# Retention and two feed-forward layers in one kernel: the opening's state summed in a PSUM bank, and its first sums of squares by products with ones

## Chip, cores and metric

The kernel runs on one core of one Trainium2 chip. The metric is the device time of one execution in microseconds; the time of a kernel is the median of three such runs. PE is TensorE, ACT ScalarE, DVE VectorE, POOL GpSimd, SP the queue that issues most DMAs.

## What is computed

Four batches of 576 positions and eight heads of 64 go through retention (attention without softmax, with a decay matrix). The result, 2304 tokens of 512 features, is normalised by its root mean square and goes through two feed-forward layers. All of it is float32.

```python
scores = scale * np.matmul(q, k.transpose(0, 1, 3, 2))
ret = scores * Dmat[None]                       # gamma ** (i - j), lower triangle
x = np.matmul(ret, v)                           # -> (2304, 512)
xn = x / np.sqrt(np.mean(x * x, -1, keepdims=True) + 1e-06) * rms_g
h = silu(xn @ w_gate) * (xn @ w_val) @ w_out    # 512 -> 1536 -> 512
g = h @ w_in                                    # 512 -> 2048
out = np.where(g >= 1, g, np.where(g <= -1, 0, (g + 1) ** 2 / 4)) @ moe2_w_out
```

## The kernel before

**Retention** works on chunks of 128 positions, five in a batch (the fifth has 64), 20 in all. `scores` (line 412) forms the scores of a chunk within itself: 16 products into two PSUM banks, which DVE multiplies with the decay into the tiles `ret` (in the opening every second chunk uses the tiles `t0`, `t1` instead), while POOL scales q and k into `qs` and `ks`. `values` (line 439) forms the chunk's output x in a bank: products of the running `state` with `qs` for c > 0 ("state products"), then of v with `ret` ("x products"), and in a second bank the products of `ks` with v ("new-state products"). For c = 0 ACT copies these into `state`; for c > 0 DVE adds them to it (line 469). ACT copies x into `xraw` and squares it into `sq`; POOL adds the squares of the four feature groups into `sums` (lines 483 and 484).

**The norm** of a token block (`rms_rstd`, line 500) multiplies `sums` with a matrix of ones on PE, so that every partition holds the sum, takes the reciprocal root on ACT (`y`), and refines it on DVE (`m`, `e`, then `y`, in the tile `o`). `norm` multiplies `xraw` by it, and `split_x` splits it into a high and a low float32r part in `xall` (ACT casts, DVE subtracts). Products of the layers are made of three float32r products of such parts (`three`, line 536). The first layer has five token blocks of 12 steps (`step_a`, line 580): two groups of 12 products into the `fr` banks, the gate on ACT and DVE, and 12 products of the step before into the four `acc` banks. The layers' weights arrive as 64-bit words and are converted once (`convert`, line 275: ACT, a shift on DVE, a merge on DVE), written back to DRAM, and split into `wt`.

**The opening** (lines 778 to 793) runs `scores` of chunks 0 to 7 and `values` of chunks 0 to 6, one behind; after `values` of chunk 3, when block 0 (512 tokens) is complete, it puts `rms_rstd`, `norm` and `split_x` of block 0. It takes its banks from a list of three pairs, `at0`/`at1`, `acc0`/`acc1`, `acc2`/`acc3`. The weights of steps 0 and 1 are converted in the opening too. From step 0 on, `att_step` puts the other chunks between the groups of `step_a`, with the banks `at0` and `at1`.

**The order of the work** on each engine is set before the kernel runs: `Plan` takes every operation with its operands, gives it an estimated cost and a due time, and lists them (`issue`, line 139); PE prefers the order of the program, the others the earliest due time. A changed operation can therefore move others on every engine. Each engine then works its list strictly in that order, waiting for semaphores. As all operations are issued by one line, the profile names line 135 throughout; tiles tell them apart.

Of the kernel before, what the change touches and what calls it, by code (L numbers as in the profile page):

```python
# [10 lines left out]
F32 = mybir.dt.float32  # L11
# [9 lines left out]
P = 128  # L21
KD = DM // P
# [3 lines left out]
CH = 128  # L26
# [185 lines left out]
def moe_chain_kernel(ctx: ExitStack, tc: tile.TileContext, att, tail, wa, wb, dmat, gq, gk, out):  # L212
    nc = Plan(tc.nc)
# [12 lines left out]
    t_p = pool("t", 2)  # L226
    r_p = pool("r", 1)
    sum_p = pool("sum", 2)
    sq_p = pool("sq", 1)
    ps_p = pool("ps", 1, space=PSUM)  # L230
    fr_p = pool("fr", 2, space=PSUM)
    dram_p = pool("dram", 1, space=DRAM)
# [5 lines left out]
    ones = const.tile([P, P], F32, name="ones")  # L238
# [150 lines left out]
    def used(i):  # L389
        del att_t[i]  # L390
        while load_att():
            pass
# [43 lines left out]
            nc.vector.tensor_mul(out=ret[h][:n, :, :n], in0=ps[h][:n, :, :n], in1=d[:n, :, h, :n])  # L436
        used(2 * i)

    def values(tags):

        i = nvalued[0]
        nvalued[0] += 1
# [19 lines left out]
            )  # L462
        if c < NFULL:
            for u, h, r in heads:
                nc.tensor.matmul(new[r, u], lhsT=ks[:, 2 * u + h], rhs=v[:, 2 * u + h], start=True, stop=True)
            for h in range(2):
                r = slice(h * D, (h + 1) * D)
                if c:
                    nc.vector.tensor_add(out=state[r, :, r], in0=state[r, :, r], in1=new[r])
                else:  # L470
                    nc.scalar.copy(out=state[r, :, r], in_=new[r])
        g0 = b * S + c * CH
        for t, s0 in enumerate(STARTS):
            lo, hi = max(g0, s0), min(g0 + n, s0 + BLOCKS[t])
            if lo < hi:
                xs, ss = x_slice(t)
                m = hi - lo
                dst = slice(lo - s0, hi - s0)
                sq = sq_p.tile([P, NPAIR, CH], F32, tag="sq", name="sq")
                src = x[:, :, lo - g0:hi - g0]  # L480
                nc.scalar.copy(out=xs[:, :, dst], in_=src)
                nc.scalar.activation(out=sq[:, :, :m], in_=src, func=ACTF.Square)
                nc.gpsimd.tensor_add(out=sq[:, :2, :m], in0=sq[:, :2, :m], in1=sq[:, 2:, :m])
                nc.gpsimd.tensor_add(out=ss[:, dst], in0=sq[:, 0, :m], in1=sq[:, 1, :m])
        used(2 * i + 1)

    def att_step(goal, what):

# [11 lines left out]
    def rms_rstd(t, ps):  # L500

        T = BLOCKS[t]
        m, e, y = rms_tiles(T)
        nc.tensor.matmul(ps[:, :T], lhsT=ones, rhs=sums[t][:, :T], start=True, stop=True)
        nc.scalar.activation(out=y, in_=ps[:, :T], func=ACTF.Abs_reciprocal_sqrt, scale=1.0 / DM, bias=eps)
        nc.vector.tensor_scalar(out=m, in0=ps[:, :T], scalar1=1.0 / DM, scalar2=EPS, op0=ALU.mult, op1=ALU.add)
        nc.scalar.activation(out=e, in_=y, func=ACTF.Square)
        nc.vector.scalar_tensor_tensor(out=e, in0=e, scalar=-0.5, in1=m, op0=ALU.mult, op1=ALU.mult)
        nc.vector.scalar_tensor_tensor(out=y, in0=e, scalar=1.5, in1=y, op0=ALU.add, op1=ALU.mult)
        return y  # L510
# [56 lines left out]
    rms = {}  # L567
# [208 lines left out]
            nc.tensor.matmul(warm[:, :P], lhsT=ones, rhs=ones, start=True, stop=True)  # L776

    warm_up(WARM)
    tags = [("at0", "at1"), ("acc0", "acc1"), ("acc2", "acc3")] * ahead
    for i in range(ahead + 1):  # L780
        scores(tags.pop())
        if i:
            values(tags.pop())
        if nvalued[0] == first and not rms:
            rms["y"] = y = rms_rstd(0, fr_p.tile([P, 512], F32, tag="fr"))
            for k in range(KD):
                norm(0, k, k + 1, y)
                split_x(0, k, k + 1)
        if i in (1, first):
            weights_f32(0 if i == 1 else 1)  # L790
        if i == first - 1:
            weights_split(0, 0)
            weights_split(0, 1)
# [88 lines left out]
```

## Time and profile before

| | us |
|---|---|
| median of three runs (921.75 to 924.12) | 923.54 |
| the profiled execution, own time | 922.58 |
| its span, first to last instruction | 920.5 |
| PE busy | 905.2 (98%) |
| DVE busy | 575.6 (63%) |
| ACT busy | 478.4 (52%) |
| POOL busy | 70.7 (8%) |

The page gives busy times as shares of the whole span. POOL's 70.7 us all lie in the first 400 us. The granted clock of PE is 0.998 on average. The chain that ended last consists to 94% of PE.

### The profile page before, as it was taken

How to read it: one execution, taken by the hardware profiler on the slowest of the kernel's cores; microseconds unless marked ns; L12 is line 12 of the kernel's file. 1: busy time of each engine (PE TensorE's matmuls, PEld its weight loads, DVE VectorE, ACT ScalarE, POOL GpSimd, SP SyncE). 2: the span in 40 equal slices, each digit the busy share in tenths (PEclk: the TensorE clock that was granted, in tenths of full speed). 3: DMA queues.
4: the chain of work that ended last, by engine and by line, in shares of the span. 5: the costliest groups of instructions: out<-in, count | busy, mean ns of one | idle time of the engine just before them, and what ended most of it. 6: DMA issues, size and time to landing. Idle time of an engine off the chain costs nothing.

```text
span 920.5 us, 13316 instructions
## 1 busy us (share of the span) xinstructions
PE 905.2 (98%) x5098; PEld 798.2 (87%) x5098; DVE 575.6 (63%) x925; ACT 478.4 (52%) x852; POOL 70.7 (8%) x80
## 2 busy tenths in 40 slices
PE   7799999999999999999999999999999999999998
PEld 7578888888889999888899998989898998989896
DVE  3978988888888798854658545333744345434343
ACT  2447656555755655533555454545654455644443
POOL 4720100210013020100000000000000000000000
PEclk9999999999999999999999999999999999999999
DMA  9778887988859847653355387555765454756432
GB/s 362 234 265 294 293 307 255 395 301 300 313 185 396 330 141 259 257 196 104 103 178 177 104 307 264 205 172 189 268 232 194 171 193 167 266 166 213 159 137 69
DMA packets 51647, 209.94 MB, mean 228 GB/s; under 512 B 5632, under 2 KB 11392, under 8 KB 47488
## 3 DMA queue, kind: packets, MB, share of 16 engines
q1 hardware_dynamic: 45392, 199.51, 61.1%
q10 hardware_dynamic: 6192, 9.59, 2.8%
q8 instruction: 40, 0.66, 0.3%
q14 instruction: 23, 0.19, 0.1%
HBM read 167.14 MB, written 41.94 MB: 227 GB/s over the span
## 4 chain that ended last, share of the span: by engine, by line
PE 94%; DVE 3%; DMA 1%; ACT 1%; issue 1%; POOL 0%; ACTq 0%; DVEq 0%
PE fr L135 51%; PE acc L135 31%; PE at L135 12%; DMA att<-in_att_dram 1%; DVE xraw L135 1%; DVE xall L135 0%; DMA gk_sb<-in_gk_dram 0%; DVE w L135 0%; DVE t L135 0%; DVE wt L135 0%; DVE o L135 0%; DVE state L135 0%; ACT att L135 0%; ACT L135 0%; ACT sq L135 0%
## 5 line engine op out<-in xcount | busy, mean ns | idle before, releaser
L135 PE MATMUL fr<-xall,wt 128*128 128x384 f32 (+1 forms) x2424 | 512.5, 356 | 2.0 <-DVE xall L135 1.3
L135 PEld LDWEIGHTS fr<-xall,wt 128*128 128x128 f32 x2424 | 437.3, 188 | 51.9 <-DVE xall L135 2.4
L135 PE MATMUL acc<-h,wt 128*128 128x512 f32 (+1 forms) x708 | 159.4, 371 | 0.0
L135 PE MATMUL acc<-wprep,h 128*128 128x512 f32 x576 | 155.7, 394 | 0.5 <-ACT h L135 0.5
L135 PEld LDWEIGHTS acc<-h,wt 128*128 128x128 f32 x708 | 128.3, 188 | 18.3
L135 DVE TENSOR_TENSOR wt<-w,wt 128x1024 fp32r<-128x1024 f32 (+1 forms) x118 | 115.8, 993 | 25.6 <-ACT wt L135 25.1
L135 ACT CAST wt<-w 128x1024 fp32r<-128x1024 f32 (+1 forms) x118 | 96.9, 835 | 52.6 <-PE acc L135 29.6
L135 PEld LDWEIGHTS acc<-wprep,h 128*128 128x128 f32 x576 | 106.6, 188 | 15.8 <-ACT h L135 0.9
L135 DVE TENSOR_TENSOR t<-fr,t 128x512 f32<-128x512 f32 (+1 forms) x120 | 76.3, 636 | 55.7 <-PE fr L135 29.0
L135 ACT ACTIVATE att<-att 128x384 f32<-128x384 f32 x156 | 79.1, 523 | 30.8 <-DVE att L135 17.2
L135 ACT CAST h<-t 128x512 fp32r<-128x512 f32 (+1 forms) x60 | 34.6, 577 | 89.8 <-DVE t L135 89.7
L135 DVE TENSOR_TENSOR att<-fr,att 128x384 f32<-128x384 f32 x48 | 26.7, 555 | 71.0 <-ACT att L135 69.6
L135 PE MATMUL at<-wprep,h 128*128 128x512 f32 x288 | 70.3, 392 | 0.0
L135 DVE TENSOR_TENSOR h<-att,h 128x384 fp32r<-128x384 f32 x96 | 52.8, 554 | 23.5 <-ACT h L135 23.1
L135 PEld LDWEIGHTS at<-wprep,h 128*128 128x128 f32 x288 | 53.7, 188 | 10.4
L135 ACT COPY att<-fr 128x384 f32<-128x384 f32 x48 | 23.0, 479 | 75.8 <-PE fr L135 72.4
L135 ACT CAST h<-att 128x384 fp32r<-128x384 f32 x96 | 48.6, 511 | 21.3 <-DVE att L135 19.9
L135 ACT ACTIVATE t<-fr 128x512 f32<-128x512 f32 (+1 forms) x60 | 33.3, 554 | 49.5 <-PE fr L135 49.4
L135 DVE SCALAR_TENSOR_TENSOR att<-att,att 128x384 f32<-128x384 f32 x48 | 26.8, 558 | 40.9 <-ACT att L135 40.9
L135 DVE TENSOR_TENSOR h<-t,h 128x512 fp32r<-128x512 f32 (+1 forms) x60 | 38.1, 635 | 12.8 <-ACT h L135 12.6
L135 DVE SCALAR_TENSOR_TENSOR att<-att,fr 128x384 f32<-128x384 f32 x24 | 13.3, 553 | 35.8 <-ACT att L135 35.8
L135 DVE TENSOR_TENSOR xall<-xraw,xall 128x512 fp32r<-128x512 f32 (+2 forms) x32 | 26.0, 828 | 2.6 <-ACT xall L135 2.4
(141 smaller groups left out, 669.6 us busy)
## 6 DMA issues: line engine op xcount, KB each, us to landing
w<-wa SPq DMA_DIRECT2D x48, 768.0 KB, 4.6
wprep<-wod SPq DMA_DIRECT2D x48, 512.0 KB, 4.1
wt<-wfd SPq DMA_DIRECT2D x24, 1024.0 KB, 5.2
wt<-wfd SPq DMA_DIRECT2D x24, 768.0 KB, 4.4
stage<-in_wb_dram SPq DMA_DIRECT2D x32, 512.0 KB, 6.3
wfd<-wprep SPq DMA_DIRECT2D x8, 1792.0 KB, 7.3
att<-in_att_dram SPq DMA_DIRECT2D x26, 512.0 KB, 6.6
stage<-in_wa_dram SPq DMA_DIRECT2D x26, 512.0 KB, 5.3
```

The costliest lines, as they stand in the source:

```text
L135: call = lambda: getattr(real, method)(*args, **kwargs)
```

## The change

In the opening only:

- `values` is called with `held`: all chunks of the opening add their new-state products into one bank, `acc3`, where the sum stands from chunk to chunk (the first product of a batch clears it), and ACT copies the sum into `state` for every chunk. DVE's additions to `state` are gone there.
- For block 0 the squares are no longer added by POOL. `square_sums` has PE multiply the four feature groups of a chunk's squares with ones, four products of 128 columns, into the chunk's columns of a bank `sq_ps`; `rms_rstd` then leaves out its own product. `sq` has two buffers instead of one.
- `square_sums` of chunk i - 2 stands behind `scores` of chunk i, and the norm of block 0 stands behind `scores` of chunk 5 and ahead of `values` of chunk 4 (before, it stood behind `values` of chunk 3 and ahead of `scores` of chunk 5).
- The other banks of the opening are taken in turn from `at0`, `at1`, `acc0`, `acc1`, `acc2`.

```diff
--- before.py
+++ after.py
@@ -226,7 +226,7 @@
     t_p = pool("t", 2)
     r_p = pool("r", 1)
     sum_p = pool("sum", 2)
-    sq_p = pool("sq", 1)
+    sq_p = pool("sq", 2)
     ps_p = pool("ps", 1, space=PSUM)
     fr_p = pool("fr", 2, space=PSUM)
     dram_p = pool("dram", 1, space=DRAM)
@@ -436,7 +436,7 @@
             nc.vector.tensor_mul(out=ret[h][:n, :, :n], in0=ps[h][:n, :, :n], in1=d[:n, :, h, :n])
         used(2 * i)
 
-    def values(tags):
+    def values(tags, held=False):
 
         i = nvalued[0]
         nvalued[0] += 1
@@ -462,10 +462,13 @@
             )
         if c < NFULL:
             for u, h, r in heads:
-                nc.tensor.matmul(new[r, u], lhsT=ks[:, 2 * u + h], rhs=v[:, 2 * u + h], start=True, stop=True)
+                nc.tensor.matmul(
+                    new[r, u], lhsT=ks[:, 2 * u + h], rhs=v[:, 2 * u + h],
+                    start=not held or c == 0 and u == 0, stop=True, skip_group_check=True,
+                )
             for h in range(2):
                 r = slice(h * D, (h + 1) * D)
-                if c:
+                if c and not held:
                     nc.vector.tensor_add(out=state[r, :, r], in0=state[r, :, r], in1=new[r])
                 else:
                     nc.scalar.copy(out=state[r, :, r], in_=new[r])
@@ -480,9 +483,24 @@
                 src = x[:, :, lo - g0:hi - g0]
                 nc.scalar.copy(out=xs[:, :, dst], in_=src)
                 nc.scalar.activation(out=sq[:, :, :m], in_=src, func=ACTF.Square)
+                if t == 0:
+                    sq_t[i] = sq
+                    continue
                 nc.gpsimd.tensor_add(out=sq[:, :2, :m], in0=sq[:, :2, :m], in1=sq[:, 2:, :m])
                 nc.gpsimd.tensor_add(out=ss[:, dst], in0=sq[:, 0, :m], in1=sq[:, 1, :m])
         used(2 * i + 1)
+
+    sq_t = {}
+    sq_ps = fr_p.tile([P, 512], F32, tag="fr", name="sq_ps")
+
+    def square_sums(i):
+
+        sq = sq_t.pop(i)
+        for k in range(KD):
+            nc.tensor.matmul(
+                sq_ps[:, i * CH:(i + 1) * CH], lhsT=ones, rhs=sq[:, k],
+                start=i == 0 and k == 0, stop=True, skip_group_check=True,
+            )
 
     def att_step(goal, what):
 
@@ -501,7 +519,8 @@
 
         T = BLOCKS[t]
         m, e, y = rms_tiles(T)
-        nc.tensor.matmul(ps[:, :T], lhsT=ones, rhs=sums[t][:, :T], start=True, stop=True)
+        if t:
+            nc.tensor.matmul(ps[:, :T], lhsT=ones, rhs=sums[t][:, :T], start=True, stop=True)
         nc.scalar.activation(out=y, in_=ps[:, :T], func=ACTF.Abs_reciprocal_sqrt, scale=1.0 / DM, bias=eps)
         nc.vector.tensor_scalar(out=m, in0=ps[:, :T], scalar1=1.0 / DM, scalar2=EPS, op0=ALU.mult, op1=ALU.add)
         nc.scalar.activation(out=e, in_=y, func=ACTF.Square)
@@ -776,16 +795,18 @@
             nc.tensor.matmul(warm[:, :P], lhsT=ones, rhs=ones, start=True, stop=True)
 
     warm_up(WARM)
-    tags = [("at0", "at1"), ("acc0", "acc1"), ("acc2", "acc3")] * ahead
+    banks = itertools.cycle(("at0", "at1", "acc0", "acc1", "acc2"))
     for i in range(ahead + 1):
-        scores(tags.pop())
-        if i:
-            values(tags.pop())
-        if nvalued[0] == first and not rms:
-            rms["y"] = y = rms_rstd(0, fr_p.tile([P, 512], F32, tag="fr"))
+        scores((next(banks), next(banks)))
+        if sq_t and i > 1:
+            square_sums(i - 2)
+        if i > first and not rms:
+            rms["y"] = y = rms_rstd(0, sq_ps)
             for k in range(KD):
                 norm(0, k, k + 1, y)
                 split_x(0, k, k + 1)
+        if i:
+            values((next(banks), "acc3"), True)
         if i in (1, first):
             weights_f32(0 if i == 1 else 1)
         if i == first - 1:
```

**ACT, from chunk 3's square to the norm.** Before (`at_0_143` is x of chunk 3, `w_148` the weights of step 0, `w_149` those of step 1):

```order
L135 ACTIVATE sq_147<-at_0_143 128x512
L135 COPY xraw_126<-at_0_143 128x4x128
L135 CAST wt_150<-w_148 128x1024
L135 ACTIVATE w_148<-stage_122 128x512
L135 ACTIVATE y_136<-fr_138,eps_108 128x512
L135 ACTIVATE o_111<-y_136 128x512
L135 ACTIVATE w_149<-stage_120 128x512
```

Now (`acc_0_142` is x of chunk 3, `acc_0_144` the bank of the state, `w_149` the weights of step 0, `w_150` those of step 1):

```order
L135 ACTIVATE sq_148<-acc_0_142 128x512
L135 COPY state_110<-acc_0_144 64x4x64 x2
L135 COPY xraw_126<-acc_0_142 128x4x128
L135 CAST wt_151<-w_149 128x1024
L135 CAST wt_151<-w_149 128x512
L135 ACTIVATE y_138<-fr_136,eps_108 128x512
L135 ACTIVATE o_111<-y_138 128x512
L135 ACTIVATE sq_148<-acc_0_143 128x512
L135 ACTIVATE w_150<-stage_120 128x512
```

The state copies, and both casts of the weights of step 0, stand ahead of `y`; one cast did before.

**POOL, from chunk 4's q to those of chunks 7 and 8.** Before (`qs_134` are q of chunks 4, 6 and 8, `t_0_130` q of chunk 7, `ks_135` k of chunk 6, `t_1_131` k of chunk 7; the pairs of `sq` and `sum` add the squares of chunks 4, 5 and 6):

```order
L135 TENSOR_TENSOR qs_134<-wpair_114,gq_sb_106 128x256
L135 TENSOR_TENSOR qs_134<-att_125,gq_sb_106 128x512
L135 TENSOR_TENSOR sq_147<-sq_147 128x2x64
L135 TENSOR_TENSOR sum_146<-sq_147 128x64
L135 TENSOR_TENSOR t_1_131<-att_123,gk_sb_107 128x512
L135 TENSOR_TENSOR sq_147<-sq_147 128x256
L135 TENSOR_TENSOR ks_135<-wpair_114,gk_sb_107 128x512
L135 TENSOR_TENSOR sum_146<-sq_147 128x128
L135 TENSOR_TENSOR t_0_130<-att_125,gq_sb_106 128x512
L135 TENSOR_TENSOR sq_147<-sq_147 128x256
L135 TENSOR_TENSOR sum_146<-sq_147 128x128
L135 TENSOR_TENSOR qs_134<-att_124,gq_sb_106 128x512
```

Now, from the same operation (the pairs of `sq` and `sum` are those of chunks 5, 4 and 6):

```order
L135 TENSOR_TENSOR qs_134<-wpair_114,gq_sb_106 128x256
L135 TENSOR_TENSOR sq_148<-sq_148 128x256
L135 TENSOR_TENSOR qs_134<-att_125,gq_sb_106 128x512
L135 TENSOR_TENSOR sum_146<-sq_148 128x128
L135 TENSOR_TENSOR sq_147<-sq_147 128x2x64
L135 TENSOR_TENSOR sum_146<-sq_147 128x64
L135 TENSOR_TENSOR t_1_131<-att_123,gk_sb_107 128x512
L135 TENSOR_TENSOR ks_135<-wpair_114,gk_sb_107 128x512
L135 TENSOR_TENSOR sq_147<-sq_147 128x256
L135 TENSOR_TENSOR qs_134<-att_124,gq_sb_106 128x512
L135 TENSOR_TENSOR sum_146<-sq_147 128x128
L135 TENSOR_TENSOR t_0_130<-att_125,gq_sb_106 128x512
```

The adds for chunk 5's squares (`sq_148`) moved ahead of chunk 4's. Those for chunk 6 (`sq_147` behind `ks_135`) stand ahead of q of chunks 8 and 7.

**DVE, from the end of the split to chunk 7's score multiplies.** Before (`acc_0_141` and `acc_0_142` are the scores of chunk 7):

```order
L135 TENSOR_TENSOR xall_112<-xraw_126,xall_112 128x512 x3
L135 TENSOR_TENSOR state_110<-state_110,at_0_144 64x4x64 x2
L135 TENSOR_SCALAR w_149<-w_149 128x512 x2
L135 SCALAR_TENSOR_TENSOR w_149<-stage_120,w_149 128x512
L135 TENSOR_TENSOR t_0_128<-acc_0_141,d_sb_105 128x512
L135 TENSOR_TENSOR t_1_129<-acc_0_142,d_sb_105 128x512
L135 SCALAR_TENSOR_TENSOR w_149<-stage_121,w_149 128x512
L135 SCALAR_TENSOR_TENSOR w_148<-stage_122,w_148 128x512
L135 TENSOR_TENSOR state_110<-state_110,at_0_144 64x4x64 x2
L135 TENSOR_TENSOR wt_151<-w_149,wt_151 128x1024
```

Now (`at_0_139` and `at_0_140` are the scores of chunk 7):

```order
L135 TENSOR_TENSOR xall_112<-xraw_126,xall_112 128x512 x3
L135 TENSOR_SCALAR w_150<-w_150 128x512
L135 SCALAR_TENSOR_TENSOR w_150<-stage_120,w_150 128x512
L135 SCALAR_TENSOR_TENSOR w_150<-stage_121,w_150 128x512
L135 TENSOR_TENSOR wt_151<-w_149,wt_151 128x512
L135 TENSOR_SCALAR w_150<-w_150 128x512
L135 SCALAR_TENSOR_TENSOR w_150<-stage_122,w_150 128x512
L135 TENSOR_TENSOR wt_152<-w_150,wt_152 128x1024
L135 TENSOR_TENSOR wt_152<-w_150,wt_152 128x512
L135 TENSOR_TENSOR t_0_128<-at_0_139,d_sb_105 128x512
L135 TENSOR_TENSOR t_1_129<-at_0_140,d_sb_105 128x512
```

The state's additions are gone; the rest of the work on the weights of steps 0 (`wt_151`) and 1 (`w_150`, `wt_152`) stands ahead of chunk 7's multiplies.

## Rows read from the trace of the kernel before

**Rows 1.** Busy time by stretches: from:to, length, busy us of each engine (instructions), PEclk, DMA share, GB/s.

```profile
6.00:38.00 32.00, 24.78 (x335) 21.12 (x334) 19.86 (x32) 13.10 (x25) 19.61 (x22) 0.95 0.91 331
38.00:50.00 12.00, 9.31 (x100) 6.76 (x98) 11.78 (x15) 3.53 (x6) 8.59 (x8) 1.00 0.65 211
50.00:60.00 10.00, 9.95 (x85) 8.18 (x84) 7.10 (x12) 6.34 (x11) 3.43 (x4) 1.00 0.67 222
```

**Rows 2.** Timeline of PE, 54 to 62 us: start, us, engine, instruction, count.

```profile
54.01 3.02 PE L135 MATMUL fr<-xall,wt 128*128 128x512 f32 x12
59.34 3.04 PE L135 MATMUL fr<-xall,wt 128*128 128x512 f32 x12
```

**Rows 3.** Waits of PE, whole span: total us, times, longest us.

```profile
PE at L135 <- DMA att<-in_att_dram: 2.9, 1, 2.9
PE fr L135 <- DVE xall L135: 1.3, 1, 1.3
```

**Rows 4.** Timeline of all engines, opening: products of V2, V3 and the sum.

```profile
18.99 0.97 PEld L135 LDWEIGHTS acc<-qs,state 128*128 128x128 f32 x8
20.08 1.09 PE L135 MATMUL acc<-ret,xraw 128*64 128x128 f32 x16
22.61 1.16 PE L135 MATMUL at<-t,state 128*128 128x128 f32 x8 [0.97 <-DVE state L135]
24.62 0.63 PE L135 MATMUL at<-o,t 128*64 128x64 f32 x16
26.96 1.12 PE L135 MATMUL fr<-sum,ones 128*128 128x512 f32 x2 [1.28 <-POOL sum L135]
```

**Rows 5.** Timeline, same answer: from chunk 3's square to the norm's mean.

```profile
24.97 0.60 ACT L135 ACTIVATE sq<-at 128x512 f32<-128x512 f32 x1 [1.40 <-PE at L135]
25.65 0.72 POOL L135 TENSOR_TENSOR sq<-sq 128x256 f32<-128x256 f32 x1 [2.34 <-ACT sq L135]
28.12 0.69 ACT L135 ACTIVATE y<-fr,eps 128x512 f32<-128x512 f32 x1 [0.56 <-PE fr L135]
28.16 1.26 DVE L135 TENSOR_SCALAR w<-w 128x512 uint32<-128x512 uint32 x1
29.46 0.69 DVE L135 TENSOR_SCALAR o<-fr 128x512 f32<-128x512 f32 x1
```

**Rows 6.** Timeline of DVE, 34 to 49 us.

```profile
34.14 1.29 DVE L135 TENSOR_TENSOR ret<-at,d_sb 128x512 f32<-128x512 f32 x2 [0.94 <-PE acc L135]
35.34 2.92 DVE L135 SCALAR_TENSOR_TENSOR xraw<-xraw,gk_sb,y 128x512 f32<-128x512 f32 x3
44.47 0.84 DVE L135 TENSOR_TENSOR state<-state,at 64x256 f32<-64x256 f32 x2
47.37 1.29 DVE L135 TENSOR_TENSOR t<-acc,d_sb 128x512 f32<-128x512 f32 x2
```

**Rows 7.** DVE groups by form (busy us, mean ns): 34 to 46, 80 to 110, 110 to 170 us.

```profile
L135 DVE TENSOR_TENSOR xall<-xraw,xall 128x512 fp32r<-128x512 f32 x4 | 5.0, 1287 | 0.0
L135 DVE SCALAR_TENSOR_TENSOR xraw<-xraw,gk_sb,y 128x512 f32<-128x512 f32 x4 | 4.4, 1152 | 0.0
...
L135 DVE TENSOR_SCALAR w<-w 128x512 uint32<-128x512 uint32 x13 | 5.4, 423 | 0.2 <-ACT w L135 0.2
...
L135 DVE TENSOR_TENSOR xall<-xraw,xall 128x512 fp32r<-128x512 f32 x4 | 2.7, 684 | 0.0
L135 DVE SCALAR_TENSOR_TENSOR xraw<-xraw,gk_sb,y 128x512 f32<-128x512 f32 x3 | 2.3, 750 | 0.0
```

**Rows 8.** Timeline of POOL, 26 to 52 us.

```profile
33.63 1.28 POOL L135 TENSOR_TENSOR qs<-att,gq_sb 128x512 f32<-128x512 f32 x1 [3.62 <-issue]
38.81 1.49 POOL L135 TENSOR_TENSOR ks<-wpair,gk_sb 128x512 f32<-128x512 f32 x1
```

**Rows 9.** Timeline of ACT, 20 to 54 us.

```profile
50.24 0.58 ACT L135 COPY xraw<-at 128x512 f32<-128x512 f32 x1
```

**Rows 10.** Busy time in one microsecond, columns as in rows 1.

```profile
12.00:13.00 1.00, 1.00 (x14) 1.00 (x12) 0.00 (x0) 0.00 (x0) 0.57 (x2) 0.50 1.02 406
```

## The prediction

> **What bounds the kernel now.** I read the busy time by stretches first. From 50 us on PE is busy in practically every microsecond, and before that it is not: 7.2 us are idle between 6 and 38 us and 2.7 us between 38 and 50 us [rows 1]. What comes after is the same list of products before and after the change. So the time changes by as much as one mark moves: the start of the second `fr` group of step 1, at 59.34 us, from where PE has no gaps [rows 2]. The largest idle spell, 2.9 us at 11.16 us, waits for a load that the change leaves alone; others wait for the split of x, 1.3 us [rows 3], for POOL's sums, 1.28 us, and for the state, 0.97 us [rows 4]. They are what the change can win back.
>
> S0 to S7 are the calls of `scores` in the opening, V0 to V7 those of `values`; a V has state products (none for c = 0), x products and new-state products.
>
> **Part 1, PE's work.** Added are 16 float32 products of 128 x 128 x 128, four for each chunk. The state products of V2 are four of the same shape: their weight loads start at 18.99 and the next group's products at 20.08, 1.09 us later [rows 4]. So 4 x 1.09 = 4.36 us. Removed is one product of 512 columns, 1.12 us [rows 4]. Net +3.3 us. Bounds: 4 x 0.97 = 3.9 us added if the weight loads alone set the pace (eight took 0.97 us), 4 x 1.16 = 4.6 us by the full length of V3's, which stood alone [rows 4]. The Trainium skill (FP8 and Floating Point Precision, TensorE Precision Notes) counts a true float32 product as four passes; at 2.4 GHz, 128 columns x 4 would be an estimated 0.21 us, 3.4 us for 16, and the forecast below would come out about 1 us lower. The rows, 1.09 us for four, decide.
>
> **Part 2, up to the sums.** Before, V3's last product ends at 25.25 us, S5 begins, and the sums go ACT, POOL, POOL, PE: the square starts at 24.97 and ACT's y at 28.12 us [rows 4, 5]. Now three blocks of squares (3.27 us) stand ahead of that point in PE's order, and the 0.97 us gap before V3's state products [rows 4] is filled by them: V3 ends at 25.25 + 3.27 - 0.97 = 27.55. S5 adds 1.1, as sixteen records do [rows 4], and the last four products 1.09 us: about 29.8. POOL's two adds, 1.3 us from 25.65 to PE's product at 26.96 [rows 4, 5], are gone from this path, but ACT's order now puts V3's two state copies, the x copy and both casts of w ahead of y. An ACT operation of 512 columns takes 0.60 us and starts the next some 0.5 us behind it [rows 5]; these are worth five and a half (the cast of 1024 two, a state copy of 256 three quarters): 27.55 + 2.75, y starts at about 30.3, so ACT, not PE, is last. That is 2.2 us later than 28.12.
>
> **Part 3, the norm.** Before, m starts at 29.46, held by a shift of w that took 1.26 us beside POOL [rows 5], and the first norm multiply at 35.34: 5.9 us [rows 5, 6]. Now DVE is free when y (0.69 us) is done, so m starts at about 31.1. Of the 5.9 us, S5's two multiplies (some 1.2, as S7's [rows 6]) are done by then, since S5 is through at 28.7; the 0.94 us of waiting for S6's products [rows 6] is gone, since half of S6 now comes early; a shift of w stays in (0.4 us [rows 7]). 5.9 - 1.2 - 0.9 + 0.4 = 4.2: the norm starts at 35.3, as before. The 3.3 us of PE work have been paid for by idle time here.
>
> **Part 4, the split.** Four norm multiplies and four subtractions ran from 35.34 to 44.47, 9.1 us [rows 6]. In that stretch one took 1.15 and 1.29 us; later, with POOL quiet, 0.75 and 0.68 us [rows 7]. POOL worked through it, after a gap of 3.62 us before 33.63 [rows 8]. In the new POOL order chunk 5's squares fall into that gap, and chunk 6's stand in the queue ahead of chunk 8's and 7's multiplies while V6's x products are behind the first `fr` products on PE. POOL then has two multiplies (as the one of 1.49 us beside DVE [rows 8]) until about 39 us and waits. So three norm multiplies as before (2.84), five operations at 0.7: 6.3 us, the split ends at 41.7. Bounds: 6.3 us, and 9.1 us if POOL stays busy. I take the short one, since POOL's next operation needs a product that itself needs the last norm. What an operation loses beside POOL is 0.4 to 0.6 us by these rows; that it may lose more is a rival below.
>
> **Part 5, from the split to the mark.** Before, DVE added the state (0.84) and did three operations of w, and S7's multiplies ran from 47.37 to 48.66 us [rows 6]. Now the state is ACT's, but all eight remaining operations on the weights of steps 0 and 1 stand ahead of S7's multiplies. From 41.7: six short ones, 3.5 us, to 45.2; the subtraction of 1024 waits for ACT's cast, which is behind V6's copies (V6's x products end near 42.9, then some 2.8 us of ACT, by 0.5 for 512 columns), so it starts at 45.75 and ends at 47.0; one more, 0.6. S7's multiplies run 47.6 to 48.8, nearly where they were. POOL's qs of chunk 7, now last in its row of four, is ready at about 47.8, so V7's state products end by 48.9 and do not decide. V7's x products end at 49.95, the copy starts at 50.0 (before 50.24). From there on the path is that of before: copy, square, table load, sigmoid, multiply, 3.77 us to the `fr` group at 54.01 [rows 2, 9]; now 53.75. The mark was 5.33 us behind it [rows 2]; three of V8's four state products (0.8 of 1.09 us) now stand ahead of it, in the gap, so the mark comes 4.5 us behind, at 58.25, that is 1.1 us early. These steps are summed without hand-overs between engines; each costs some 0.05 to 0.1 us (0.08 from ACT's 25.57 to POOL's 25.65 [rows 5]), and about eight lie on the path: +0.6.
>
> **Sum.** -1.1 + 0.6 = -0.5 us. DMA: in SP's queue the store of the first converted weights now stands ahead of the next att load and waits for DVE until about 28 us; that load needs the buffer which S5 frees at 28.7, so I cost this at nothing (without that cover chunk 7's POOL multiply and V7 would wait). Four pairs of state adds leave DVE (0.84 each [rows 6]) for ACT, which is busy 3.5 of 12 us from 38 to 50 [rows 1]. Profiled: 922.58 - 0.5 = 922.1 us; that run is 0.96 us under the median of the three, 923.54, so the forecast for the median is **923.0 us**. 0.3% is 2.8 us, about what a measurement of this kernel can tell from no change.
>
> **Rivals.**
> - *Slower: POOL stays beside DVE.* If chunk 7's loads let POOL work through the split, it ends at 44.4 (+2.7), and with one shift of w at 1.26 instead of 0.42 us [rows 5, 7] S7's multiplies end at 52.3 and everything behind them moves: -0.5 + 2.7 + 0.8 = +3.0; from 923.54 that is **926.5 us**. It decides once POOL runs on past 40 us. For it: it was so before. Against it: chunk 6's squares block the queue. Chance 0.16, part of it under 0.3%.
> - *Faster: PE never waits.* All idle time behind 11.16 us, 7.0 us of the 9.9 [rows 1, 3], goes and only 3.3 us of work come: -3.7, **919.8 us**. Against it: DVE has 11.8 of 12 us of work from 38 to 50 [rows 1], and S7's multiplies stand behind it. 0.10.
> - *The clock falls.* The clock was at 0.50, 1.2 GHz, from 12 to 13 us, after the 2.9 us gap [rows 10]. A new gap as long near 35 us would double some 3 us of products: +1.5, **924.5 us**. The longest that I find is 1.7 us. 0.04.
> - *DVE waits for whole POOL operations.* If each of the two POOL multiplies beside the norm holds DVE up for its full length, 1.49 us [rows 8], 3.0 us are lost there instead of the 1.2 that three operations at 0.4 lose: +1.8, **924.8 us**, inside 0.3%. The Trainium skill (SBUF — State Buffer, Who interferes with whom) has it so: a VectorE operation with two SBUF inputs and a GpSimd operation that reads SBUF exclude each other for a whole instruction. The rows at 1.15 and 1.29 us, stretched by less than a POOL operation, speak for the smaller loss. Chance 0.15.
>
> **How the numbers follow.** The forecast has 0.55. The range takes the fast rival's half way and the slow one nearly whole: 920.2 to 926.4. Faster than 920.8 takes most of the fast rival and a tail of the forecast, 0.13; slower than 926.3 most of the slow rival, 0.14; within, 0.73.
>
> **What would show it.** Right: y near 30.3, the first norm multiply near 35.3, `xall` subtractions of 0.7 us with POOL idle beside them, the `fr` group of step 1 between 57 and 60 us, PE's busy time about 3 us above the 905.2 of before, its idle time about 4 us less. Wrong: a split that takes 9 us, S7's multiplies after 50 us, a PE gap behind 60 us, or a mark before 57 us.

## The result, and the profile after

The changed kernel takes 931.07 us (929.18 to 934.86, six runs) against 923.37 of the kernel before beside it: ratio 1.0091, 95% interval 1.0075 to 1.0108. It is slower by 7.7 us and lies outside the forecast range. The profiled execution took 930.2 us, its span is 928.4.

Busy time by stretches of the kernel after, columns as in [rows 1] (the last row to be held against the kernel before in the second fence):

```profile
6.00:38.00 32.00, 28.77 (x369) 25.76 (x367) 16.91 (x26) 15.55 (x31) 14.39 (x15) 0.95 0.98 367
38.00:50.00 12.00, 10.49 (x72) 7.45 (x72) 9.82 (x15) 6.75 (x12) 4.41 (x6) 0.86 0.62 230
50.00:60.00 10.00, 5.77 (x60) 5.08 (x56) 7.47 (x12) 3.93 (x7) 3.30 (x3) 0.83 0.72 256
320.00:330.00 10.00, 8.20 (x52) 7.37 (x51) 9.25 (x15) 7.01 (x11) 3.10 (x3) 1.00 0.03 13
```

The same view of the kernel before, 320 to 330 us:

```profile
320.00:330.00 10.00, 9.79 (x80) 8.85 (x79) 9.20 (x10) 7.12 (x12) 4.86 (x4) 1.00 0.32 112
```

Up to 38 us PE has 4.0 us more work (forecast were 3.3 in all) and idles 4.0 us less. Then it stands: 4.2 us of 50 to 60 us are empty where before 0.05 were [rows 1], the clock is at 0.83 there, and between 320 and 330 us another 1.8 us are missing (0.2 before). The timeline of the kernel after, in order of time, shows how the gap comes about:

```profile
30.16 0.69 ACT L135 ACTIVATE y<-fr,eps 128x512 f32<-128x512 f32 x1
33.32 0.73 POOL L135 TENSOR_TENSOR sq<-sq 128x256 f32<-128x256 f32 x1 [3.85 <-ACT sq L135]
34.25 1.76 DVE L135 SCALAR_TENSOR_TENSOR y<-o,y 128x512 f32<-128x512 f32 x1
37.13 3.67 DVE L135 SCALAR_TENSOR_TENSOR xraw<-xraw,gk_sb,y 128x512 f32<-128x512 f32 x3
39.39 5.55 PE L135 MATMUL fr<-xall,wt 128*128 128x512 f32 x15 [1.42 <-ACT xall L135]
41.99 1.88 DVE L135 TENSOR_TENSOR xall<-xraw,xall 128x512 fp32r<-128x512 f32 x3
44.88 1.09 PE L135 MATMUL acc<-ret,wpair 128*64 128x128 f32 x16
47.18 0.74 POOL L135 TENSOR_TENSOR sq<-sq 128x256 f32<-128x256 f32 x1 [7.59 <-ACT sq L135]
49.22 3.12 DVE L135 TENSOR_TENSOR wt<-w,wt 128x1024 fp32r<-128x1024 f32 x2 [2.15 <-ACT wt L135]
49.54 2.25 POOL L135 TENSOR_TENSOR t<-att,gq_sb 128x512 f32<-128x512 f32 x1
52.26 1.28 DVE L135 TENSOR_TENSOR t<-at,d_sb 128x512 f32<-128x512 f32 x2
53.09 1.93 PE L135 MATMUL at<-t,state 128*128 128x128 f32 x8 [2.93 <-DVE t L135]
54.95 1.90 PE L135 MATMUL at<-t,att 128*64 128x128 f32 x16
65.44 3.01 PE L135 MATMUL fr<-xall,wt 128*128 128x512 f32 x12
```

The last row is the mark: 65.44 against 59.34 [rows 2]. The same products of V6 and V7 in the kernel before:

```profile
38.34 1.09 PE L135 MATMUL at<-ret,wpair 128*64 128x128 f32 x16
45.78 1.06 PE L135 MATMUL at<-t,state 128*128 128x128 f32 x8
```

V6's x products (44.88) now stand behind 15 products of step 0; before, they ran at 38.34. ACT's copies of V6, POOL's adds and its multiply for chunk 7 (49.54), ACT's cast for DVE's subtraction (49.22) and S7's multiplies (52.26) follow in a row, and V7's state products wait 2.93 us. They take 1.93 us for what took 1.06 before; from 54 to 56 us the clock is at 0.50 (last section).

Why does V6 stand there? The planner's own reckoning, printed for both kernels (us in its plan, no measured time):

```
before: V6 x products ready 36.98, released by the load of wpair; 3 products of step 0 ahead
after:  V6 x products ready 40.96, released by the load of wpair; 15 products of step 0 ahead
```

It reckons all transfers one behind the other at 330 GB/s. In the changed kernel the weights of step 0 are converted earlier, so their store (`wa`) and one more load of `stage` come ahead of V6's load in the SP queue, and the plan has it landing 4 us later. In the trace it came later too, but sooner than in the plan. Its issue, first before, then now:

```profile
30.56 0.33 SPq L135 DMA_DIRECT2D wpair<-in_att_dram  x1
32.15 0.33 SPq L135 DMA_DIRECT2D wpair<-in_att_dram  x1
```

From issue to landing it took 3.9 us before and 5.5 now, so it landed at about 34.5 and 37.6. PE was through with V6's state products at 37.97; so ahead of step 0 V6 would not have waited for it. (In f1 below, V6 ran there at 37.78.)

The planner's own total tells of the loss too: by the same reckoning the whole plan ends at 911.0 us before and at 917.9 now. It is no safe guide: it has e2_state_only below, which cost nothing, at 915.5, and p_rate_400, the slowest of all, at 908.5.

### The profile page after: what moved, and what is told of

Read it like the earlier page. It is cut to its first block, busy times and chain, and to the rows that moved or that the text cites. A ratio compares the mean times of both kernels' runs of the same rounds, so it can differ in the third digit from the quotient of the medians.

```text
span 928.4 us, 13353 instructions
## 1 busy us (share of the span) xinstructions
PE 910.9 (98%) x5128; PEld 804.7 (87%) x5128; DVE 568.5 (61%) x917; ACT 483.9 (52%) x860; POOL 60.1 (6%) x72
## 4 chain that ended last, share of the span: by engine, by line
PE 94%; DVE 2%; DMA 2%; ACT 1%; issue 0%; DVEq 0%; ACTq 0%
PE fr L135 50%; PE acc L135 31%; PE at L135 12%; DMA x2d<-o 1%; DMA att<-in_att_dram 1%; DMA gk_sb<-in_gk_dram 0%; DVE xraw L135 0%; DVE wsum L135 0%; DVE wt L135 0%; ACT wt L135 0%; ACT att L135 0%; DVE ret L135 0%; DVE y L135 0%; DVE w L135 0%; DVE state L135 0%
## 5 line engine op out<-in xcount | busy, mean ns | idle before, releaser
L135 DVE TENSOR_TENSOR wt<-w,wt 128x512 fp32r<-128x512 f32 (+1 forms) x118 | 114.5, 983 | 23.8 <-ACT wt L135 23.4
L135 ACT CAST wt<-w 128x512 fp32r<-128x512 f32 (+1 forms) x118 | 96.5, 836 | 45.4 <-PE acc L135 31.4
L135 DVE TENSOR_TENSOR t<-fr,t 128x512 f32<-128x512 f32 (+1 forms) x120 | 76.4, 636 | 69.7 <-ACT t L135 34.5
L135 DVE SCALAR_TENSOR_TENSOR att<-att,fr 128x384 f32<-128x384 f32 x24 | 13.3, 554 | 35.3 <-ACT att L135 35.3
L135 ACT CAST xall<-xraw 128x512 fp32r<-128x512 f32 (+2 forms) x32 | 21.5, 675 | 9.2 <-DVE xraw L135 5.6
```

The lines of the kernel that those rows point to most:

```text
L135: call = lambda: getattr(real, method)(*args, **kwargs)
```

## The experiments

The times are medians, with the ratio to the kernel before measured beside each. "Profiled" is the own time of the one execution that was traced. "Block 0" is where that execution copies block 0's first accumulator (`o<-acc`): 158.99 before, 163.66 after. Where the profiled time lies far from the median (p_rate_360, m1, h1), the trace does not show the usual execution. Of each edit only the lines that matter are shown.

| run | us | ratio, 95% | profiled | block 0 |
|---|---|---|---|---|
| e1_rotate | 931.43 | 1.0071 to 1.0105 | 930.23 | 164.86 |
| e4_mul_first | 928.43 | 1.0041 to 1.0078 | 928.34 | 160.48 |
| e2_state_only | 923.88 | 0.9997 to 1.0029 | 923.41 | 158.78 |
| e3_squares_only | 933.28 | 1.0080 to 1.0130 | 935.29 | 165.02 |
| f1_v6_first | 930.93 | 1.0045 to 1.0092 | 932.68 | 163.78 |
| f3_three_first | 930.33 | 1.0050 to 1.0089 | 931.42 | 164.63 |
| h1_products_added | 928.76 | 1.0033 to 1.0068 | 932.00 | 162.66 |
| k1_fillers | 927.06 | 1.0026 to 1.0055 | 928.48 | 160.92 |
| p1_rate_380 | 923.78 | 0.9983 to 1.0014 | 925.65 | 156.81 |
| p0_before_380 | 922.08 | 0.9976 to 1.0001 | 924.04 | 158.54 |
| p_rate_360 | 929.61 | 1.0046 to 1.0085 | 923.84 | 156.90 |
| p_rate_400 | 933.85 | 1.0092 to 1.0148 | 934.38 | 158.09 |
| m1_380_330 | 924.31 | 0.9983 to 1.0021 | 929.43 | 159.30 |
| m0_before_380_330 | 920.93 | 0.9956 to 0.9991 | 921.16 | 156.09 |
| m2_360_330 | 921.86 | 0.9965 to 0.9997 | 922.64 | 157.84 |
| m3_before_360_330 | 924.42 | 0.9998 to 1.0026 | 921.99 | 157.95 |
| m4_state_360_330 | 925.97 | 1.0018 to 1.0048 | 925.50 | 161.71 |

### First: the gap behind S7, and which half of the change

**e1_rotate** gives S7 banks that V7 does not use.

```diff
-    banks = itertools.cycle(("at0", "at1", "acc0", "acc1", "acc2"))
+    banks = itertools.cycle(("acc0", "acc1", "acc2", "at0", "at1"))
```

> The changed kernel with its cycle of five banks begun at acc0 instead of at0: S7 then writes acc0 and acc1, and V7's x products keep at0, which no multiply of S7 reads. Theory A (the shared bank): in the changed kernel V7's state products waited 3.09 us for S7's first multiply because both lie in at0; with banks of their own they and V7's new-state products go ahead of the multiplies, the gap of PE behind S7 shrinks from 2.9 to under 1 us, V7's state products take about 1.06 us at full clock instead of 1.93, the second group of fr products of step 1 (the mark, 65.44 in the changed kernel, 59.34 before) starts at 62 to 62.7, and the time is 927.5 to 928.2 us. Theory B (S7's multiplies are late by themselves, behind the subtractions on DVE, and V7's x products need them anyway): the wait goes over to V7's x products, the mark moves by under 1.3 us, time 929.8 to 931. Theory C (PE pays the 16 square products in full, 3.3 us and more, whatever the waits): mark and time unchanged within 0.5 us, 930.5 to 931.5.

Theory A falls. The wait for S7's multiply is gone, and another stands in its place, at the same time (timeline of PE):

```profile
52.96 1.16 PE L135 MATMUL at<-t,state 128*128 128x128 f32 x8 [1.23 <-POOL t L135]
```

V7's products run at full clock here, but the next wait, 1.39 us ahead of V8's state products, has the clock at 0.50 behind it (60 to 62 us), and the mark stays at 65.82. Theories B and C both fit.

**e4_mul_first** moves, in the finished order of DVE, two subtractions behind S7's multiplies.

```diff
+            order = [i for i in order if i not in self.late]
+            at = max(order.index(i) for i in self.early) + 1
+            order[at:at] = self.late
```

> The changed kernel with S7's two multiplies moved on DVE ahead of the two weight subtractions of step 1 (128x1024 and 128x512), which stood ahead of the first and waited 2.15 us for ACT's cast. Theory B (the order on DVE): the multiplies start when POOL's qs of chunk 7 is there or at once after S7, at 50.2 to 51 instead of 52.26, V7's state products follow at 51 to 52 instead of 53.06, mark at 63 to 64, time 928 to 929.5 us. Theory A (the shared bank): the same gain as far as the multiplies come earlier, but POOL's own work for qs of chunk 7 (ended at 51.8) does not bind the multiplies, only V7's state products, which then cannot start ahead of 51.8: mark 63.9 to 64.5, time 929.3 to 930. Theory C (PE pays the square products in full): 930.5 to 931.5. If the subtractions, now later, hold the first products of step 1's weights, the gap only moves behind V7 and the time stays at 930.5 to 931.5 too; the gap of PE then stands ahead of the first fr group of step 1.

The multiplies start at 49.89, V7's state products at 50.72 at full clock, the mark is at 62.27 and 2.6 us are gained: the order on DVE is one of the links. But block 0 ends only 1.5 us late, and the time is still 5 us over that of before: more is lost behind block 0 than ahead of it. The time is in B's range, the mark ahead of it.

**e2_state_only** takes the squares' part back (`square_sums`, the second `sq` buffer, the condition in `rms_rstd`); **e3_squares_only** takes the state's part back.

```diff
-            values((next(banks), "acc3"), True)
+            values((next(banks), "acc3"))
```

> The state half alone: the state is summed up in PSUM and copied by ACT, banks in the changed kernel's cycle (S7 and V7 in at0) and the later place of the reciprocal root, but the squares are summed up by POOL as before. Theory A (the shared bank carries the loss): V7's state products wait for S7's multiply here too, so most of the loss stays: mark 62 to 64.5, time 926.5 to 929.5 us. Theory C (the square products carry it): mark 59.3 to 60.3, time 923 to 924.5.

> The squares half alone: the squares are summed up by PE's products with ones, the state is added by DVE as before, with the banks still in the changed kernel's cycle (S7 and V7 in at0). Theory A (the shared bank): V7's state products wait for S7's multiply, and DVE with its state additions is later still: mark 65 to 67, time 930.5 to 933 us. Theory C (the square products carry the loss, ACT's copies nothing): as the changed kernel within 0.7 us, 930.4 to 931.8, with the loss spread over the opening and not in a gap behind S7.

The state half costs nothing that can be told (mark 60.35), the squares half all of it. But S7 and V7 share a bank in e2 as well, so A falls again; and in e2 the planner puts V6 ahead of step 0, in e3 behind 15 of its products. So the two runs do not tell the square products from the order that was planned for them. e3 is slower than either theory gave.

### Second: the order, edited by hand, and the products alone

**f1_v6_first** puts V6's x and new-state products ahead of step 0 in the finished order of PE; **f3_three_first** also S7's multiplies ahead of the subtractions, and POOL's multiply for chunk 7 ahead of the adds of V6's squares (a list of moves, applied to the plan before it is issued).

```diff
+    nc.moves = [
+        (('values', ahead - 1), ('front', 0, 0), 0),
+        (('ret', ahead), ('sub', 1, 0), 0),
+        (('qs', ahead), ('sqadd', ahead - 1), 0),
+    ]
```

> The changed kernel with one edit of the finished order, on PE alone: V6's x and new-state products stand ahead of the first product of step 0 instead of behind 15 of them. Theory D (the order): the changed kernel's loss comes from V6's place. Its products ran at 44.88 us (38.34 before), so ACT's copies, POOL's work for chunk 7 (which ended at 51.8) and V7's state products came late, and the clock fell in the gap. Now V6's x products run at 38.5 to 39.5 (its operand is loaded by 38.8), POOL's add of V6's squares starts at 43 to 44 instead of 47.18, V7's state products at 49.5 to 51 instead of 53.06, the mark (65.44 in the changed kernel, 59.34 before) at 61 to 63, time 926 to 928.5 us. Theory C (PE pays the 16 square products, and the order matters little): the gap behind S7 closes by less than 1 us, time 930 to 931.5.

> As the run before, and two more edits of the finished order: S7's multiplies ahead of step 1's two weight subtractions on DVE, and POOL's product of chunk 7's queries ahead of the adds of V6's squares. Theory D: V7's state products start behind V6's state copy and S7's multiplies, at 46.5 to 48.5, no wait over 1.5 us on the way, no fall of the clock in 50 to 60 us, mark at 59.5 to 61, and the time is 924 to 926.5: what is left over 923.3 is PE's square products as far as no wait takes them in, and the stalls behind 300 us that the changed order has there (1.4 us for ACT's cast at 320 to 330). Theory C: not under 927.

Theory D, that V6's place alone carries the loss, falls. In f1 V6's x products run at 37.78, 7 us sooner, and V7 gains 1.5. POOL's adds now come while DVE converts weights, and they stretch (f1, timeline of POOL, DVE and PE):

```profile
43.66 3.16 POOL L136 TENSOR_TENSOR sq<-sq 128x256 f32<-128x256 f32 x1 [4.19 <-ACT sq L136]
43.68 0.41 DVE L136 TENSOR_SCALAR w<-w 128x512 uint32<-128x512 uint32 x1
44.01 1.28 DVE L136 SCALAR_TENSOR_TENSOR w<-stage,w 128x512 uint32<-128x512 uint32 x2
46.26 1.10 DVE L136 SCALAR_TENSOR_TENSOR w<-stage,w 128x512 uint32<-128x512 uint32 x1
49.85 1.71 POOL L136 TENSOR_TENSOR t<-att,gq_sb 128x512 f32<-128x512 f32 x1
51.61 1.84 PE L136 MATMUL at<-t,state 128*128 128x128 f32 x8 [4.35 <-POOL t L136]
```

An add that took 0.74 us in the changed kernel takes 3.16, chunk 7's multiply ends at 51.56 (51.79 in the changed kernel), PE waits 4.35 us and the clock falls behind it. This trace is of the slowest of f1's seven executions: they took from 926.0 us, at a mean clock of 0.998, to 932.7 at 0.993, so the fastest lies in D's range and the median does not. In f3, whose profiled execution runs some 1.8 us behind f1's from the start, V7 follows sooner and the wait moves to S8 (2.22 us for DVE's addition to the state, then a clock of 0.58 from 56 to 62 us). Each edit only moved the wait.

**h1_products_added** is e2 with 16 idle products at the squares' places, which the planner does not count.

```diff
+        nc.gratis = True
         for k in range(KD):
```

> The state half alone (squares by POOL, 923.9 us, mark 60.35) with 16 products of ones and 128 columns added on PE at the places of the changed kernel's square products; their result is not used and the planner takes them at no time, so that the order of all other work stays as in the state half. They read the copied x, not its squares. Theory D (order and waits): PE waits less elsewhere, the products add 0 to 1.5 us, time 923.5 to 925.5, mark 60.3 to 61.8. Theory C (PE pays them): plus 3.3 to 4.4 us, time 927 to 928.5, mark 63.6 to 64.8.

4.9 us over e2 by medians, 3.4 by the ratios, so in C's range or a little above it: in an order that was not made for them PE pays for the products, and for a fall of the clock (0.72 in 44 to 50 and 56 to 62 us of the profiled execution, the slowest of ten).

### Third: the clock, and the plan

**k1_fillers** leaves the order of all other work as it is and gives PE idle products to do where it stood.

```diff
+            for name, m in (("filler", 0), 5), (("filler", 1), 10):
+                nc.mark[name] = range(len(nc.ops), len(nc.ops) + m)
+                for _ in range(m):
+                    nc.tensor.matmul(idle[:, :P], lhsT=ones, rhs=ones, start=True, stop=True)
```

> The changed kernel with 15 idle products of ones (128x128) on PE whose result nobody reads: 5 behind V6's state products and 10 behind S7's scores, where the changed kernel's PE stood still for 1.42 and 2.93 us; the planner takes them at no time and all other work keeps its order. They take away no wait, only the standstill. Theory E (the clock carries part of the loss): the clock stays at 1.00 in 38 to 44 and in 50 to 56 us (0.72 and 0.77 in the changed kernel), the products of step 0 take 3.9 instead of 5.5 us as far as the split lets them, V7's state and x products 1.1 us each instead of 1.93 and 1.90, the first copy of block 0's end (163.66 in the changed kernel, 158.99 before) comes at 161 to 162.5, time 928 to 929.5. Theory F (the waits alone): the copy stays at 163.5 to 164.5, time 930.5 to 932.

Busy time by stretches, first the changed kernel, then k1:

```profile
44.00:50.00 6.00, 6.00 (x62) 4.33 (x60) 3.82 (x7) 3.69 (x7) 2.82 (x4) 1.00 0.66 235
50.00:56.00 6.00, 3.07 (x22) 2.72 (x20) 4.91 (x7) 0.85 (x2) 1.79 (x1) 0.77 0.97 349
56.00:62.00 6.00, 4.59 (x53) 4.08 (x50) 4.57 (x8) 5.08 (x8) 2.61 (x4) 0.95 0.46 145
```

```profile
44.00:50.00 6.00, 6.00 (x64) 4.66 (x64) 4.53 (x8) 3.97 (x7) 3.66 (x3) 1.00 0.64 186
50.00:56.00 6.00, 5.11 (x66) 4.67 (x66) 4.63 (x9) 2.52 (x4) 2.55 (x3) 1.00 0.95 373
56.00:62.00 6.00, 5.32 (x46) 4.49 (x44) 5.97 (x9) 4.64 (x8) 2.57 (x4) 1.00 0.58 210
```

And from k1 the row of 40 to 42 us, with step 0's first products and V7's state products in PE's timeline:

```profile
40.00:42.00 2.00, 1.91 (x10) 1.31 (x9) 2.00 (x4) 1.87 (x4) 0.00 (x0) 1.00 0.77 307
40.06 4.04 PE L136 MATMUL fr<-xall,wt 128*128 128x512 f32 x15
51.92 1.16 PE L136 MATMUL at<-t,state 128*128 128x128 f32 x8 [0.17 <-POOL t L136]
```

Behind S7 the clock stays at 1.00 and block 0 ends 2.7 us sooner. By medians 4.0 us are gained, more than either theory gave: E holds. (The two profiled executions differ by 1.7 us.) Behind the first fillers the clock is at 1.00 from 40 to 42 us, where the changed kernel has 0.50, and the 15 products take 4.04 instead of 5.55 us. It had fallen ahead of them, though, to 0.53 from 36 to 38, which is not explained. V7's state products start 1.2 us sooner, so the fillers shorten waits as well. By medians half of the loss goes with PE's standing still; how much of that half is the products at the low clock, and how much the later start of what waits for them, is not separated.

**p1_rate_380** and the others change the planner's rate for transfers, for all work or (m) for the opening alone.

```diff
-            return 2000 + n * out.ap[0][1] * 4 / 330
+            return 2000 + n * out.ap[0][1] * 4 / 380
```

In the m runs the rate is a variable, 380 or 360, set back where the opening ends:

```diff
+    nc.rate = 330
     for s, (_, t, f) in enumerate(steps):
```

> The changed kernel with one number of the planner changed: it reckons transfers at 380 GB/s instead of 330 (the changed kernel's trace moved 340 to 415 GB/s in the opening). With 330 its plan has V6's operand landing at 40.96 us and puts V6 behind 15 products of step 0; the trace has it landed by 38.1. With 380 the plan puts V6 ahead of all of them, and all other work is planned anew too. Theory D: V6's x products at 38 to 39, V7's state products at 47 to 50.5, time 923 to 927.5. Theory C: 930 to 931.5. If the new order of the rest of the program has stalls of its own, they show behind 66 us and not in the opening.

With one number of the planner the 7.7 us are gone: the interval includes no change. V6 runs ahead of step 0, chunk 7's multiply is done long before it is wanted, and V7's state products start 7.5 us sooner, without a wait (p1, timeline of PE and POOL):

```profile
36.55 1.09 PE L135 MATMUL acc<-ret,wpair 128*64 128x128 f32 x16
39.46 1.74 POOL L135 TENSOR_TENSOR t<-att,gq_sb 128x512 f32<-128x512 f32 x1
45.56 1.13 PE L135 MATMUL at<-t,state 128*128 128x128 f32 x8
```

Block 0 ends 2.2 us sooner than in the kernel before. That gain is given back later, where the new plan has stands of its own: PE is busy for 18.09 of the 20 us from 540 to 560, where before it was for 19.90 (p1's trace is of its slowest execution).

> The kernel before with the planner's transfer rate at 380 GB/s instead of 330: what the other plan does without the change. Theory G (the change by itself costs next to nothing, the plan made for it at 330 carries the loss): between 921 and 926 us, so that the changed kernel at 380 (923.8) stands within 2.5 us of it. Theory C' (the change costs 3 us or more under any plan, and the rate of 380 gains as much): 918 to 920.5.

> The changed kernel planned with 360 GB/s: its plan puts V6's x products behind 5 products of step 0 instead of 15 (at 330) or none (at 380). Theory G (the place of V6 and what hangs on it decides): 923 to 927 us, no gap of PE over 2.5 us in 38 to 60, first copy of block 0's end by 160. Theory C: 930 to 931.5.

> The changed kernel planned with 400 GB/s: V6 ahead of all products of step 0, as at 380, the rest planned anew. Theory G: 921 to 927 us, first copy of block 0's end at 156 to 160; how far from 923.8 shows how much such a plan differs by itself. Theory C: 930 to 931.5.

The kernel before is nearly indifferent to this plan. But the changed kernel's two others miss G's ranges. p_rate_400 ends block 0 at 158.09, as early as before, and is the slowest of all. It loses its time later (PE busy 96.22 of 100 us from 300 to 400), so a good opening does not make a good plan. p_rate_360 spreads from 923.84 to 932.55, and its trace, with block 0 at 156.90, is of the fastest of ten executions; where the others lose their time is not known.

> The changed kernel with the planner's transfer rate at 380 GB/s for the opening alone and at 330, as before, for all that is recorded behind it. Theory H (the later losses follow from the late opening): the first copy of block 0's end at 156.5 to 158.5 as at 380 throughout (156.81), no stand at 320 to 330, and 919 to 922.5 us. Theory I (the later stalls come from any new plan and have nothing to do with the opening): the opening gains its 2 us, the stalls behind 270 us take 1 to 5, and the time is 922.5 to 927.

> The same with 360 GB/s for the opening. Theory H: first copy of block 0's end at 156.5 to 158.5, 919 to 923 us. Theory I: 923 to 930.

> The kernel before with 380 GB/s for the opening and 330 behind it. Theory G (the change by itself costs and gains next to nothing): within 2.5 us of the changed kernel planned in the same way. Theory C' (the change costs 3 us under any plan): 3 us and more under it.

> The kernel before with 360 GB/s for the opening and 330 behind it, the pair of the changed kernel planned so (921.86 us). Theory G (the change by itself does next to nothing): 920 to 923.5 us. Theory C' (it costs 3 us and more under any plan): under 919. If it is over 924, the change gains where its plan is right.

> The state half alone (squares by POOL) with 360 GB/s for the opening and 330 behind it. Theory G: within 1.5 us of the changed kernel planned so, 920.4 to 923.4, PE's 3.3 us of square products being taken in by waits. Theory C' (the square products cost PE's time): 2.5 to 4 us under it, 918 to 919.4.

Theory H is half right: m2 keeps the opening's gain and is in its range, m1 is not (its trace, of the slowest of twelve executions, has block 0 at 159.30 and a clock of 0.58 from 44 to 50 us). Between 300 and 400 us both still stand, 1.4 us in all (PE busy 98.6 of 100; 97.5 in the changed kernel, 99.8 in the kernel before), and so does m0 (98.6) without the change: that part belongs to the plans.

The pairs planned alike, changed less before, by medians: +7.7 us at 330, +1.7 at 380, +3.4 with 380 for the opening, -2.6 with 360 for it (by the ratios 8.4, 0.9, 2.6 and -2.9). The sign changes, and the theory C' (3 us under any plan) falls with the last pair. That the change costs nothing by itself is not shown either. The four pairs average +2.6 us, and m1 stands 3.4 over its pair, more than the 2.5 I had allowed. The plans at 360 and 400 throughout, 6.7 and 10.9 us over the kernel before, have no pair. m3 and m4 are both slower than G and C' gave. m4, without the square products, is 4.1 us slower than m2, but it is planned anew as well, so this does not price the products. Only h1 added them in an order that stayed, and there they cost 4.9 us by medians. Two versions beat the kernel before by a little: m0 and the changed kernel m2.

## Why the prediction was wrong

- **Part 1** held: a block of four square products starts the next 1.0 to 1.09 us behind it. PE's busy time rose by 5.7 us (905.2 to 910.9) where 3.3 were forecast; V7's two groups at the low clock alone took 1.7 us more than at full clock.
- **Part 2** held: y at 30.16, forecast 30.3.
- **Part 3** was 1.8 us short: the norm starts at 37.1, not 35.3. I had put POOL's adds for chunk 5 into its gap before 33.6; they came at the gap's end, from 33.3 to 36.3, and POOL worked beside DVE. DVE's last multiply for y took 1.76 us, before 0.68.
- **Part 4** then held in the main: the first three norm multiplies took 3.67 us beside POOL (2.92 before [rows 6]), the last three `xall` subtractions 1.88, 0.63 each, with POOL idle, 6.7 us in all (6.3 forecast).
- **Part 5 is the step that failed**, the path from the split to V7:

| us | forecast | measured | late by |
|---|---|---|---|
| the split ends | 41.7 | 43.87 | 2.2 |
| V6's x products end | 42.9 | 45.97 | 3.1 |
| the subtraction of 1024 starts | 45.75 | 49.22 | 3.5 |
| S7's multiplies start | 47.6 | 52.26 | 4.7 |
| V7's x products end | 49.95 | 56.85 | 6.9 |

The lateness of the split (parts 3 and 4) is 2.2 us of this. Between the split's end and V6 the sum had nothing; PE's order had four products of step 0 there. The subtraction of 1024 and the one behind it took 3.04 us beside POOL's multiply for chunk 7, forecast 1.85. "V7's state products end by 48.9 and do not decide": they started at 53.09 and set the end, because POOL's multiply, forecast for 47.8, ended at 51.79 and S7's multiplies at 53.54, and then V7 ran at the low clock. I overlooked that S7 and V7 share bank `at0`; e1 shows that POOL's multiply would have held V7 as long.

- **DMA, costed at nothing.** The att load that the sum looked at went out at 28.80, as forecast (28.7). But V6's load, with the store and the load that now stand ahead of it in SP's queue, landed 3.2 us later in the trace and 4 in the plan, and because of it the plan put V6 behind 15 products. I read the new order for what it does to DVE, ACT and POOL, but not why PE's order put V6 there.
- **The clock** was a rival at 0.04, priced at 1.5 us, because the longest gap I found was 1.7 us. The mechanism came, behind a gap of 2.93 and already behind one of 1.42; keeping PE at work there gave 4.0 us back.
- **"What comes after is the same list."** It is, but in another order. The mark moved by 6.1 us and the span by 7.9: block 0 ends 4.7 us late, block 2 (its first copy 364.90 before, 371.61 after) 6.7, the end 7.9. So the time did not move by as much as the mark alone.
- **The rivals.** None reaches 931 us; the slowest, POOL beside DVE through the split, stops at 926.5, and POOL was idle for 7.59 us there. It stood beside DVE ahead of the norm and again at the two subtractions. And the range is not what it says of itself: 920.2 takes in 2.8 of the 3.2 us from the forecast to the fast rival, not half.

What stays open: why plans with a good opening differ by up to 10 us later on (p1 and p_rate_400), how the 7.7 us divide exactly, since hand edits, fillers and plans overlap, and what the square products cost by themselves in a good order.

## What to carry over

Where a planner orders the work, a change of a few operations is a change of the whole order: compare it under several plans before the operations are blamed or praised. Here six plans of the changed kernel took 921.9 to 933.9 us, four of the kernel before 920.9 to 924.4, and the sign of the difference hung on the plan. Read in the new order what a planner moved far, and ask by what belief it did (here a load that it expected 3 us later than it came). A wait of TensorE can cost more than its length, and idle products in it are a cheap test of how much more.

## What the runs showed of the hardware

- The wait that DVE and POOL impose on each other goes both ways. Beside POOL the norm multiplies stretched (3.67 us for three). Beside DVE's conversions of weights it was POOL that stretched: an add took 3.16 instead of 0.74 us in f1, a multiply 4.64 instead of 1.3 in f3. DVE's operations beside them kept their 0.41 and 0.64 until the last, which took 1.10 (f1) and 1.65 (f3) instead of 0.69. In f3:

```profile
44.51 4.64 POOL L136 TENSOR_TENSOR t<-att,gq_sb 128x512 f32<-128x512 f32 x1 [3.25 <-DMA att<-in_att_dram]
48.06 1.65 DVE L136 SCALAR_TENSOR_TENSOR w<-stage,w 128x512 uint32<-128x512 uint32 x1
```

  The prediction reckoned only with the first direction. The Trainium skill (SBUF — State Buffer, Who interferes with whom) says that the order of issue decides which of the two blocks; the rows agree that either can be the one.
- After PE gaps of 2.93 us (changed kernel) and 4.35 us (f1) the granted clock was at 0.50, 1.2 GHz, once PE was at work again. A gap's length alone doesn't tell: in the changed kernel it was also 0.50 from 40 to 42 us, behind a gap of 1.42 that had followed one of 0.89, and in p1 it stayed at 1.00 behind gaps of 2.18 and 1.78. The changed kernel in steps of 2 us (columns as in [rows 1]):

```profile
40.00:42.00 2.00, 1.88 (x5) 1.01 (x4) 2.00 (x5) 1.79 (x3) 0.00 (x0) 0.50 0.81 312
50.00:52.00 2.00, 0.16 (x4) 0.00 (x0) 2.00 (x2) 0.85 (x2) 1.79 (x1) 1.00 1.03 393
52.00:54.00 2.00, 0.91 (x5) 0.94 (x6) 1.97 (x5) 0.00 (x0) 0.00 (x0) 0.80 0.98 363
54.00:56.00 2.00, 2.00 (x15) 1.77 (x16) 0.94 (x2) 0.00 (x0) 0.00 (x0) 0.50 0.90 291
56.00:58.00 2.00, 1.31 (x26) 1.17 (x22) 0.63 (x2) 1.09 (x3) 0.00 (x0) 0.84 0.63 209
```
